# Step two of a staged transform: products laid out in PSUM with four frequencies side by side, and the fifth group's sums moved from VectorE to GpSimd

## The chip, the core and the metric

The kernel runs on one core of one Trainium2 chip. A core has five engines that run side by side, each with its own queue: TensorE (PE in the profile, with PEld for its weight loads), VectorE (DVE), ScalarE (ACT), GpSimd (POOL) and SyncE (SP, which here issues most DMAs). TensorE writes its results to PSUM; DVE and ACT read and write PSUM and SBUF; POOL is used on SBUF only. The metric is the device time of the whole program in microseconds (us), taken as the median of several runs; smaller is better.

## What is computed

The input is 2048 tokens by 640 channels. Two blocks are applied, each with a normalisation and a modulation ahead of it and a gated residual behind it. The change touches the first block only, a long causal convolution per channel that the reference does with an FFT:

```python
k_shift = sum over 4 taps of k_pad[:, t:t+S, :] * shift_k[:, ks-1-t]
kv  = k_shift * v
kv_f = rfft(pad(kv, S));  kf_f = rfft(pad(ssm_k, S))
y   = irfft(kv_f * kf_f)[:S] + kv * ssm_D
x   = x + ga * (h * y)          # h: normalised, modulated x
...
h = layernorm(x) * (1 + cb) + sb
x = x + gb * (w2^T gelu(w1^T layernorm(h) + b1) + b2)   # over the token axis
```

The product of the two spectra, `kv_f * kf_f`, is a complex product: for each frequency and channel, (a + ib)(c + id) gives a real part ac - bd and an imaginary part ad + bc.

## The kernel before

The second block (a token MLP, which fills the time from about 292 us on) is a long run of matmuls and is not touched. The first block goes over the channels in five chunks of 128 (the loop `for c in range(NC)`, line 524 on). In each chunk the transform of length 2048 is done as two small dense transforms, each a set of matmuls, and back again with two more:

- `step1(side, t)` (line 222): first transform, one call for each of four quarters t and for each of two sides (0: kv, 1: the filter). It writes PSUM, and ACT copies the result into the SBUF tile `T_z` (line 235).
- `f2(g)` (line 239): **step two**, called for eight groups g of eight frequencies k1. For each frequency (kk), each of two results (ri: real, imaginary) and each half h of the partitions there is one matmul at line 249: the weight is 128x64 from `W2`, the moving operand is 64 columns of `T_z` in 32 pairs, the pairs 1 KiB apart; of the 64 result columns the first 32 belong to kv (s = 0) and the last 32 to the filter (s = 1). That makes 32 matmuls a group, 256 a chunk and 1280 in the program; the profile has two MATMUL records and two LDWEIGHTS records for each (these operands are f32), so 64 a group, 512 a chunk, 2560 in all. The two halves h write different partitions of the same columns.
- Behind the matmuls of a group ACT copies the filter's part into an SBUF tile `kt` (line 253, one of two). `mul()` then makes two DVE instructions of 512 elements a partition: `pa` = kv's part times `kt`, `pb` = kv's part times `kt` with real and imaginary swapped. Both read kv's part straight from PSUM and write the SBUF tile `P`, whose two halves of 1024 serve even and odd groups. `add()` makes two instructions of 256 elements: a difference over `pa` for the real part, a sum over `pb` for the imaginary part, both written to `Y`.
- `i2(r)` (line 271) and `i1(half)` (line 289) transform back. `i2` reads `Y`, and so waits for the sums of all eight groups.

What sets the order around the change is the loop over g, written by hand. Iteration g issues the matmuls and the ACT copy of group g, then `mul` of group g - 1, then `add` of group g - 2, then some other DVE work (the four taps of a later chunk, `kv_ops`, one instruction at a time from a list). The sums go to POOL, with two exceptions. In chunks 2 and 3, iteration 6 gives its sums (those of group 4, the fifth of eight) to DVE. In chunks 1 to 4 the last group's sums are cut in two halves of 128 elements and go to DVE as well. Behind the loop stand two calls of `step1` for the next chunk, then `i2(0)`.

Two pools of storage tie the engines together. PSUM has three rotating buffers of 1024 words a partition (`psum()`, line 71), so the matmuls of group g + 3, or the next `step1`, can start only when both DVE products of group g have read theirs. And a half of `P` can be written by `mul` of group g only when the sums of group g - 2 have read it. All elementwise instructions of two inputs go through the helper at line 60, so in the profile they all carry that line, and are told apart by tile names: `p<-pst,kt` is a product, `y<-p` a sum, `kt<-in,tap`, `tap<-tap,kt` and `x<-tap,in` are the taps.

In the layout before, a matmul writes 64 neighbouring words. A group's 1024 words a partition are ordered (kk, ri, s, i) with i the 32 columns of a side, so ACT and DVE read PSUM in runs of 32 words, and the sums, which write `Y` as (i, k) with eight k in a row, read `P` one word at a time with 64 words (256 bytes) from one to the next.

Of the kernel before, what the change touches and what calls it, by code (L numbers as in the profile page):

```python
# [11 lines left out]
AF = mybir.ActivationFunctionType  # L12
ALU = mybir.AluOpType
# [37 lines left out]
def mixer_kernel(ctx: ExitStack, tc: tile.TileContext, q, k, v, shift_k, ssm_k, ssm_D, w1, b1, w2, b2, c,  # L51
# [7 lines left out]
    act, dve, pool, pe, sync = nc.scalar, nc.vector, nc.gpsimd, nc.tensor, nc.sync  # L59
    TT = lambda eng, o, a, b, op: eng.tensor_tensor(o, a, b, op=op)  # L60
    uid = [0]

    def mem(tag, n, name=None):

        return sb.tile([128, n], F32, name=name or tag, tag=tag, bufs=1)
# [5 lines left out]
    def psum(slot=None):  # L71

        uid[0] += 1
        slot = ring[uid[0] % len(ring)] if slot is None else slot
        return psp.tile([128, 1024], F32, name=f"pst_{uid[0]}", tag=f"pst{slot}", bufs=1)

    def dram(t, offset, ap):
        return bass.AP(tensor=t.tensor, offset=t.offset + offset, ap=ap)
# [20 lines left out]
    Y = T_y.rearrange("p (r i k) -> p r i k", r=2, i=32)  # L99
    W2 = [t.rearrange("p (k m) -> p k m", m=64) for t in T_w2]  # L100
# [6 lines left out]
    def lay_w2(i, n):  # L107

        k, e = slice(32 * (n // 2), 32 * (n // 2) + 32), n % 2
        act.activation(W2[i][:, k, 32 * e:32 * e + 32], W2C[i][:, k], AF.Copy, scale=MK[:, e:e + 1])  # L110
# [59 lines left out]
    def perm_add(c, eng=pool):  # L170
        for h in range(2):
            r = KSR[64 * h:64 * h + 1].rearrange("p (i n) -> p i n", i=64)[:, :, 0]
            TT(eng, r, r, DR[64 * h:64 * h + 1], ALU.add)
# [65 lines left out]
    def f2(g):  # L239

        ps = psum()
        for kk in range(8):
            k1 = 8 * g + kk
            for ri in range(2):
                for h in range(2):
                    o = 128 * kk + 64 * ri
                    rhs = bass.AP(tensor=T_z.tensor, offset=T_z.offset + 128 * h + 2 * k1,
                                  ap=[T_z.ap[0], [256, 32], [1, 2]])
                    pe.matmul(ps[64 * h:64 * h + 64, o:o + 64], W2[k1 // 32][:, 2 * (k1 % 32) + ri], rhs, start=True, stop=True)  # L249
        pv = ps.rearrange("p (m s i) -> p m s i", s=2, i=32)  # L250
        xs_ = pv[:, :, 0]
        kt = KT[g % 2]
        act.activation(kt.rearrange("p (m i) -> p m i", i=32), pv[:, :, 1], AF.Copy)  # L253
        pa, pb = P[:, 1024 * (g % 2):1024 * (g % 2) + 512], P[:, 1024 * (g % 2) + 512:1024 * (g % 2) + 1024]
        m16 = lambda t: t.rearrange("p (m i) -> p m i", i=32)

        def mul():
            TT(dve, m16(pa), xs_, m16(kt), ALU.mult)
            sw = bass.AP(tensor=kt.tensor, offset=kt.offset + 32, ap=[kt.ap[0], [64, 8], [-32, 2], [1, 32]])
            TT(dve, pb.rearrange("p (k r i) -> p k r i", k=8, r=2), xs_.rearrange("p (k r) i -> p k r i", r=2), sw,  # L260
               ALU.mult)

        def add(eng=pool, parts=(slice(0, 32),)):
            for i in parts:
                for ri, t, op in ((0, pa, ALU.subtract), (1, pb, ALU.add)):
                    t = t.rearrange("p (k r i) -> p r i k", k=8, r=2)
                    TT(eng, Y[:, ri, i, 8 * g:8 * g + 8], t[:, 0, i], t[:, 1, i], op)
        return mul, add


# [18 lines left out]
    def i1(half, slot=None):  # L289

        ps = psum(slot)
        for jj in range(8):
            for ri in range(2):
                for e in range(2):
                    p = slice(64 * e, 64 * e + 64)
                    for b in range(2):
                        n2 = 16 * b + 8 * half + jj
                        pe.matmul(ps[64 * b:64 * b + 64, 512 * e + 64 * jj:512 * e + 64 * jj + 64],  # L298
                                  V1[p, ri, n2], T2[p, :, 32 * ri + n2], start=ri == 0, stop=ri == 1)
        return ps  # L300
# [118 lines left out]
    def split_rows(r, t, blocks, hi=True, lo=True):  # L419
        j, t = slice(4 * r, 4 * r + 4), t.rearrange("p (j m) -> p j m", j=4)  # L420
        for f in blocks if hi else ():
            act.activation(blk[f][0][:, j].bitcast(F32R), t[:, :, 128 * f:128 * f + 128], AF.Copy)
        for f in blocks if lo else ():
            TT(dve, blk[f][1][:, j].bitcast(F32R), t[:, :, 128 * f:128 * f + 128], blk[f][0][:, j], ALU.subtract)
# [86 lines left out]
    def load_q():  # L511
        for j in range(16):
            for b in range(2):
                sync.dma_start(XH[j // 8][64 * b:64 * b + 64, j % 8], dram(q, (16 * b + j) * D, [[32 * D, 64], [1, D]]))
        for kk in range(4):
            mod_load(0, kk, (T_v1[:, 0:1920], T_v1[:, 1920:3840], T_aux[:, 0:1920], T_aux[:, 2048:3968])[kk])
# [3 lines left out]
    def dv(n):  # L520
        for _ in range(min(n, len(fill))):
            fill.pop(0)()

    x1s = lambda c, j: lambda: dve.bn_stats(bst[:, j, c, :], XR(j, DC * c, DC))
    for c in range(NC):
        cn = c + 1 if c + 1 < NC else None
        ac, po = a1_ops(c)
        pend_m = pend_a = None
        for g in range(8):
            m_, a_ = f2(g)  # L530
            if pend_m:
                pend_m()
            if pend_a:
                pend_a(dve if c in (2, 3) and g == 6 else pool)
            pend_a, pend_m = (pend_m and pa_next), m_
            pa_next = a_
            if c:
                for f_ in ac[2 * g:2 * g + 2]:
                    f_()
            if cn is None and g < 4:  # L540

                act.activation(X[:, 512 * g:512 * g + 1], epsc, AF.Copy)
                for b in range(2):
                    sync.dma_start(X[64 * b:64 * b + 64, 512 * g:512 * g + 512],
                                   dram(w1, (16 * b + g) * F, [[32 * F, 64], [1, 512]]))
            if c == 0 and g < 4:
                lay_w2(1, g)
                if g == 3:
                    load_q()
            if cn is None:  # L550
                dv(4 if g else len(fill) - 16)
                if g == 5:
                    t = mem("w0", 4096, "wb0")
                    blk[0] = j16(t[:, 0:2048]), j16(t[:, 2048:4096])
                if g in (5, 7):
                    split_rows(1, T_aux[:, 0:2048], (0,), g == 5, g == 7)
            else:
                dv(-(-len(fill) // max(6 - g, 1)))
            if c and cn is not None and g == 3:
                perm_add(cn)  # L560
# [16 lines left out]
        if c == 0:  # L577
# [3 lines left out]
            ps = psum()  # L581
# [45 lines left out]
        else:  # L627
            t = mem("w1", 4096, "wb1")
# [6 lines left out]
            t = mem("in", 4288, "wb3")  # L635
# [4 lines left out]
        if c:  # L640
# [3 lines left out]
            if cn is None:  # L644
# [5 lines left out]
                t = mem("y", 4096, "wb2")  # L650
# [20 lines left out]
        for half in range(2):  # L671
            ps = i1(half)
# [33 lines left out]
    start = []  # L706
# [91 lines left out]
    ps = i1(1, s1)  # L798
# [227 lines left out]
    for f_ in FS:  # L1026
# [12 lines left out]
        ps = psum().rearrange("p (h m) -> p h m", h=2)  # L1039
# [117 lines left out]
def build(inputs):  # L1157
    import concourse.bacc as bacc

    nc = bacc.Bacc("TRN2", target_bir_lowering=False, num_devices=1)  # L1160
    arrays, args = {}, []

    def add(name, a):
        a = np.ascontiguousarray(a)
        arrays[f"in_{name}_dram"] = a
        args.append(nc.dram_tensor(f"in_{name}_dram", a.shape, mybir.dt.from_np(a.dtype), kind="ExternalInput").ap())

    for name in _INS:
        a = np.asarray(inputs[name])
        add(name, a.reshape(S, D) if name in ('A_q', 'A_k', 'A_v') else a)  # L1170
    for name, a in _constants().items():
        add("const_" + name, a)
    args.append(nc.dram_tensor("out_0_dram", (S, D), F32, kind="ExternalOutput").ap())
    with tile.TileContext(nc) as tc:
        mixer_kernel(tc, *args)
    return nc, arrays
# [8 lines left out]
```

## Time and profile before

| what | value |
|---|---|
| median of 3 runs | 682.18 us (678.96 to 683.72) |
| the profiled execution, its own time | 679.36 us |
| its span, first to last instruction | 677.6 us |
| mean granted TensorE clock | 0.990 |
| busy: PE, DVE, ACT, POOL | 629.8, 513.0, 316.0, 143.4 us |
| the five chunks of the first block | about 23 to 292 us |

The profiled execution is 2.82 us below the median of the runs, and 1.76 us of its time lie outside the span. A line of the profile's groups gives line, engine, operation, output<-input tiles, partitions x elements and count, then the busy time, the mean duration in ns of one, and the idle time of the engine just before them with what ended it. A timeline line gives start, length, engine, line, operation, tiles, shape, count, and in brackets how long the engine had been idle before it and who released it. Matmul durations overlap, so the rate of matmuls is read from starts and stretches, not from the duration of one.

### The profile page before, as it was taken

What the parts mean: (1) busy time and instruction counts of PE and PEld (TensorE: products, weight loads), DVE (VectorE), ACT (ScalarE), POOL (GpSimd) and SP (SyncE); (2) the same over time, 40 slices, a digit from 0 to 9 for tenths busy, and PEclk for the clock granted to TensorE, in tenths of its full rate; (3) what the DMA queues carried; (4) which work ended last, traced back from release to release, by engine and by line L of the source; (5) the groups of instructions that cost most, each with busy time, mean ns of one, the idle gap of its engine ahead of it and who ended that gap; (6) DMA issues with size and microseconds to landing.
All of it is one profiled execution on the core that took longest, in us unless ns stands there. A gap on an engine that the chain in (4) does not pass through costs nothing.

```text
span 677.6 us, 20710 instructions
## 1 busy us (share of the span) xinstructions
PE 629.8 (93%) x9057; PEld 611.8 (90%) x9057; DVE 513.0 (76%) x862; ACT 316.0 (47%) x483; POOL 143.4 (21%) x116
## 2 busy tenths in 40 slices
PE   0699888999999999889999999999999999999997
PEld 0699678999989989668999999999999999999997
DVE  7677689979978757879993312854679888888886
ACT  0574674745645546557875223433334333333331
POOL 5298039526327228200000000000000000000000
PEclk9999989999999999979999999999999999999999
DMA  9977987655432522634005540686499554355601
GB/s 188 217 219 237 369 147 152 156 95 136 85 69 86 165 63 69 180 86 102 2 1 108 116 88 1 166 221 172 143 345 304 176 178 121 114 160 167 182 34 40
DMA packets 173552, 95.91 MB, mean 142 GB/s; under 512 B 89715, under 2 KB 163222, under 8 KB 173462
## 3 DMA queue, kind: packets, MB, share of 16 engines
q1 hardware_dynamic: 168914, 93.28, 52.9%
q10 hardware_dynamic: 4548, 1.31, 1.1%
q8 instruction: 71, 1.16, 0.7%
q14 instruction: 19, 0.16, 0.1%
HBM read 77.53 MB, written 17.04 MB: 140 GB/s over the span
## 4 chain that ended last, share of the span: by engine, by line
PE 69%; DVE 17%; POOL 3%; issue 3%; DMA 3%; SPq 3%; ACT 2%; ACTq 0%; DVEq 0%; POOLq 0%
PE pst L1086 25%; PE pst L445 17%; PE pst L230 9%; PE pst L249 6%; PE pst L279 5%; PE pst L951 3%; DVE tap L60 3%; PE pst L298 2%; POOL y L60 2%; DVE p L60 2%; DVE kt L60 2%; SPq L166 1%; DVE x L60 1%; DMA in<-in_A_k_dram 1%; POOL t L60 1%
## 5 line engine op out<-in xcount | busy, mean ns | idle before, releaser
L249 PEld LDWEIGHTS pst<-z,w 128*64 128x64 f32 x2560 | 94.8, 141 | 5.8 <-ACT z L235 3.3
L249 PE MATMUL pst<-z,w 128*64 128x64 f32 x2560 | 96.1, 240 | 4.1 <-ACT z L235 2.1
L60 POOL TENSOR_TENSOR y<-p 128x256 f32<-128x256 f32 x68 | 89.4, 1366 | 25.6 <-DVE p L60 25.3
L230 PE MATMUL pst<-v,x 128*64 128x128 f32 x640 | 46.0, 303 | 25.4 <-DVE x L60 23.3
L230 PEld LDWEIGHTS pst<-v,x 128*64 128x64 f32 x640 | 43.9, 220 | 26.2 <-POOL t L470 23.2
L235 ACT ACTIVATE z<-pst 128x1024 f32<-128x1024 f32 (+2 forms) x45 | 46.5, 1046 | 41.8 <-PE pst L230 24.1
L60 DVE TENSOR_TENSOR p<-pst,kt 128x512 f32<-128x512 f32 x80 | 52.0, 692 | 15.2 <-ACT kt L253 8.7
L253 ACT ACTIVATE kt<-pst 128x512 f32<-128x512 f32 x40 | 25.3, 633 | 44.7 <-PE pst L249 25.3
L279 PEld LDWEIGHTS pst<-v,y 32*128 32x128 f32 x1280 | 38.7, 190 | 5.8 <-issue 3.9
L279 PE MATMUL pst<-v,y 32*128 32x64 f32 x1280 | 40.4, 275 | 3.2 <-issue 2.3
L230 PE MATMUL pst<-v,p 128*64 128x128 f32 x640 | 36.7, 274 | 2.4 <-ACT p L176 1.8
L230 PEld LDWEIGHTS pst<-v,p 128*64 128x64 f32 x640 | 35.0, 137 | 2.9 <-ACT p L176 1.9
L1086 PE MATMUL pst<-r_z,m_w 128*128 128x320 f32 x198 | 37.2, 309 | 0.0
L60 DVE TENSOR_TENSOR tap<-tap,kt 128x512 f32<-128x512 f32 x51 | 35.6, 697 | 1.3
L60 DVE TENSOR_TENSOR kt<-in,tap 128x512 f32<-128x512 f32 x51 | 35.1, 688 | 1.5
L1086 PEld LDWEIGHTS pst<-r_z,m_w 128*128 128x128 f32 x198 | 31.1, 188 | 0.1
L287 ACT ACTIVATE z<-pst 128x512 f32<-128x512 f32 x38 | 21.4, 664 | 19.6 <-PE pst L279 19.5
L1023 ACT ACTIVATE m_w<-m_v 128x896 fp32r<-128x896 f32 x19 | 17.9, 948 | 23.2 <-DVE m_v L60 13.1
L298 PEld LDWEIGHTS pst<-z,v 64*64 64x64 f32 x1280 | 23.0, 148 | 5.3 <-issue 2.5
L298 PE MATMUL pst<-z,v 64*64 64x64 f32 x1280 | 24.8, 233 | 1.9 <-issue 1.1
L855 ACT ACTIVATE pst<-pst,sm 128x640 f32<-128x640 f32 x14 | 10.7, 766 | 32.5 <-PE pst L445 32.5
L60 DVE TENSOR_TENSOR m_w<-m_v,m_w 128x896 fp32r<-128x896 f32 x19 | 20.6, 1087 | 6.5 <-ACT m_w L1023 6.5
(302 smaller groups left out, 1435.5 us busy)
## 6 DMA issues: line engine op xcount, KB each, us to landing
x<-in_B_w_dram SPq DMA_DIRECT2D x18, 512.0 KB
m_v<-in_B_w_dram SPq DMA_DIRECT2D x20, 384.0 KB
aux<-in_A_ssm_k_dram SPq DMA_DIRECT2D x10, 512.0 KB
out_dram<-m_w SPq DMA_DIRECT2D x32, 160.0 KB
in<-in_A_k_dram SPq DMA_DIRECT2D x36, 128.0 KB
in<-in_A_v_dram SPq DMA_DIRECT2D x36, 128.0 KB
ts<-m_p SPq DMA_DIRECT2D x10, 320.0 KB
m_w<-xs SPq DMA_DIRECT2D x20, 160.0 KB
```

Of the source, the lines that this page charges most:

```text
L60: TT = lambda eng, o, a, b, op: eng.tensor_tensor(o, a, b, op=op)
L230: pe.matmul(ps[64 * ri:64 * ri + 64, o:o + 128], lhs, F1[:, 128 * ri:128 * ri + 128], start=True, stop=True)
L235: act.activation(Z[:, side, t, :, k0:k1].rearrange("p a k e -> p e a k"), ps.rearrange("p (e a k) -> p e a k", a=8, e=2)[:, :, :, k0:k1], ...
L249: pe.matmul(ps[64 * h:64 * h + 64, o:o + 64], W2[k1 // 32][:, 2 * (k1 % 32) + ri], rhs, start=True, stop=True)
L253: act.activation(kt.rearrange("p (m i) -> p m i", i=32), pv[:, :, 1], AF.Copy)
L279: pe.matmul(pp[qd // 2][:, o:o + 64], Y[p, ri, i:i + 2].rearrange("p i k -> p (i k)"), V2[p, 64 * ri:64 * ri + 64], start=ri == 0, stop=ri ...
L287: act.activation(o, i, AF.Copy)
L298: pe.matmul(ps[64 * b:64 * b + 64, 512 * e + 64 * jj:512 * e + 64 * jj + 64], V1[p, ri, n2], T2[p, :, 32 * ri + n2], start=ri == 0, stop=r ...
L445: pe.matmul(ps[0:m, h, 0:320], w_.bitcast(F32R), r_[:, 320 * h:320 * h + 320].bitcast(F32R), start=first and i == 0, stop=last and i == 2)
L951: pe.matmul(ps[n][:, h, 0:320], sets[n][:, j].bitcast(F32R), r[:, 320 * h:320 * h + 320].bitcast(F32R), start=j == 0 and r is hh, stop=j = ...
L1023: act.activation(W[n][0].bitcast(F32R), A[p, w_], AF.Copy)
L1086: pe.matmul(bank[n], w[:, i].bitcast(F32R), r.bitcast(F32R), start=m == 0 and k == 0, stop=m == 6 and k == 2)
```

## The change

The words of a group in PSUM are put in another order: (b, s, r, i, k), where b is the bank of 512 words, s the side, r real or imaginary, i the column, and k the four frequencies of that bank, innermost. Bank b holds the frequencies 4b to 4b + 3. A matmul now writes its 64 words one by one, four words (16 bytes) apart, in two rows of 32 that are 256 words apart. ACT and DVE read PSUM in runs of 256 words, the products lie in `P` in the same order, and the sums read `P` in runs of 128 words and write `Y` in runs of four words where they wrote runs of eight. The matmuls, their order, weights and moving operands stay as they are, and so do the number and size of the copies and products. The second edit takes the exception of chunks 2 and 3 out: group 4's sums go to POOL there too.

```diff
@@ f2(g)
         ps = psum()
+        pk = ps.rearrange("p (b s r i k) -> p b r k s i", b=2, s=2, r=2, i=32)
         for kk in range(8):
             k1 = 8 * g + kk
             for ri in range(2):
                 for h in range(2):
-                    o = 128 * kk + 64 * ri
                     rhs = bass.AP(tensor=T_z.tensor, offset=T_z.offset + 128 * h + 2 * k1,
                                   ap=[T_z.ap[0], [256, 32], [1, 2]])
-                    pe.matmul(ps[64 * h:64 * h + 64, o:o + 64], W2[k1 // 32][:, 2 * (k1 % 32) + ri], rhs, start=True, stop=True)
-        pv = ps.rearrange("p (m s i) -> p m s i", s=2, i=32)
+                    pe.matmul(pk[64 * h:64 * h + 64, kk // 4, ri, kk % 4], W2[k1 // 32][:, 2 * (k1 % 32) + ri], rhs,
+                              start=True, stop=True)
+        pv = ps.rearrange("p (b s m) -> p b s m", b=2, s=2)
         xs_ = pv[:, :, 0]
         kt = KT[g % 2]
-        act.activation(kt.rearrange("p (m i) -> p m i", i=32), pv[:, :, 1], AF.Copy)
+        halves_ = lambda t: t.rearrange("p (b m) -> p b m", b=2)
+        act.activation(halves_(kt), pv[:, :, 1], AF.Copy)
         pa, pb = P[:, 1024 * (g % 2):1024 * (g % 2) + 512], P[:, 1024 * (g % 2) + 512:1024 * (g % 2) + 1024]
-        m16 = lambda t: t.rearrange("p (m i) -> p m i", i=32)
         def mul():
-            TT(dve, m16(pa), xs_, m16(kt), ALU.mult)
-            sw = bass.AP(tensor=kt.tensor, offset=kt.offset + 32, ap=[kt.ap[0], [64, 8], [-32, 2], [1, 32]])
-            TT(dve, pb.rearrange("p (k r i) -> p k r i", k=8, r=2), xs_.rearrange("p (k r) i -> p k r i", r=2), sw,
+            TT(dve, halves_(pa), xs_, halves_(kt), ALU.mult)
+            sw = bass.AP(tensor=kt.tensor, offset=kt.offset + 128, ap=[kt.ap[0], [256, 2], [-128, 2], [1, 128]])
+            TT(dve, pb.rearrange("p (b r m) -> p b r m", b=2, r=2), xs_.rearrange("p b (r m) -> p b r m", r=2), sw,
                ALU.mult)
         def add(eng=pool, parts=(slice(0, 32),)):
             for i in parts:
                 for ri, t, op in ((0, pa, ALU.subtract), (1, pb, ALU.add)):
-                    t = t.rearrange("p (k r i) -> p r i k", k=8, r=2)
-                    TT(eng, Y[:, ri, i, 8 * g:8 * g + 8], t[:, 0, i], t[:, 1, i], op)
+                    t = t.rearrange("p (b r i k) -> p r b i k", b=2, r=2, i=32)[:, :, :, i]
+                    TT(eng, Y[:, ri, i, 8 * g:8 * g + 8].rearrange("p i (b k) -> p b i k", b=2), t[:, 0], t[:, 1], op)
@@ loop over g
             if pend_a:
-                pend_a(dve if c in (2, 3) and g == 6 else pool)
+                pend_a()
```

What moves can be seen on two engines. On DVE, at the end of step two of chunk 2 before the change, where pst_2296, 2337, 2384 and 2424 are the PSUM buffers of groups 4 to 7:

```order
L60 TENSOR_TENSOR p<-pst_2296,kt 128x512 x2
L60 TENSOR_TENSOR x<-tap,in 128x512
L60 TENSOR_TENSOR p<-pst_2337,kt 128x512 x2
L60 TENSOR_TENSOR y<-p 128x32x8 x2
L60 TENSOR_TENSOR p<-pst_2384,kt 128x512 x2
L60 TENSOR_TENSOR p<-pst_2424,kt 128x512 x2
L60 TENSOR_TENSOR y<-p 128x16x8 x4
```

The same place on DVE after the change:

```order
L60 TENSOR_TENSOR p<-pst_2296,kt 128x512 x2
L60 TENSOR_TENSOR x<-tap,in 128x512
L60 TENSOR_TENSOR p<-pst_2337,kt 128x512 x2
L60 TENSOR_TENSOR p<-pst_2384,kt 128x512 x2
L60 TENSOR_TENSOR p<-pst_2424,kt 128x512 x2
L60 TENSOR_TENSOR y<-p 128x2x16x4 x4
```

Group 4's two sums no longer stand between the products of groups 5 and 6, and the last group's four half sums keep their place with another shape. On POOL, chunk 2 from the end of chunk 1's additions to its own sums, before the change (aux<-aux,rows is a small addition of one row, the rest y<-p are sums):

```order
L60 TENSOR_TENSOR xa<-xa,aux 128x8x128
L60 TENSOR_TENSOR xb<-xb,aux 128x8x128
L60 TENSOR_TENSOR y<-p 128x32x8 x4
L60 TENSOR_TENSOR aux<-aux,rows 1x64 x2
L60 TENSOR_TENSOR y<-p 128x32x8 x8
```

The same place on POOL after the change:

```order
L60 TENSOR_TENSOR xa<-xa,aux 128x8x128
L60 TENSOR_TENSOR xb<-xb,aux 128x8x128
L60 TENSOR_TENSOR y<-p 128x2x32x4 x4
L60 TENSOR_TENSOR aux<-aux,rows 1x64 x2
L60 TENSOR_TENSOR y<-p 128x2x32x4 x10
```

POOL has two sums more in the chunk, ten in place of eight behind the small addition; chunk 3 moves alike, and POOL has 72 sums in the program in place of 68.

## The prediction

> **What bounds the kernel now.** I read the page's busy times first, then the five stretches of step two, then what TensorE waits for around them, then the timeline at one of those waits. The page's first part says that TensorE is busy nearly all the time:
>
> ```profile
> PE 629.8 (93%) x9057; PEld 611.8 (90%) x9057; DVE 513.0 (76%) x862; ACT 316.0 (47%) x483; POOL 143.4 (21%) x116
> ```
>
> That share is a mean over stages, so the next view is line 249 alone in its five stretches, chunk by chunk (stretch; its length; PE and weight-load busy time with counts; clock; DMA share; GB/s):
>
> ```profile
> 41.24:60.20 18.96, 18.96 (x512) 18.90 (x512) 1.00 0.80 228
> 102.26:124.12 21.86, 19.84 (x512) 19.18 (x512) 1.00 0.78 160
> 152.84:171.70 18.86, 18.86 (x512) 18.86 (x512) 1.00 0.55 132
> 202.03:220.90 18.87, 18.87 (x512) 18.87 (x512) 1.00 0.35 103
> 251.92:270.90 18.98, 18.98 (x512) 18.91 (x512) 1.00 0.29 80
> ```
>
> In four of the five stretches busy time equals length: TensorE runs step two's 512 records back to back in 18.9 us, at full clock, and is the bound there. Only chunk 1 has holes, 21.86 - 19.84 = 2.02 us. So neither the sums on POOL nor the products on DVE set the pace of step two now. They can cost time only where TensorE waits, and these are all of its waits from 100 to 290 us (us in total, times, longest):
>
> ```profile
> PE pst L279 <- issue: 2.3, 1, 2.3
> PE pst L230 <- DVE p L60: 2.1, 2, 1.1
> PE pst L249 <- DVE p L60: 2.0, 3, 0.7
> PE pst L249 <- ACT z L235: 1.7, 4, 0.4
> PE pst L298 <- issue: 1.1, 2, 0.9
> PE pst L230 <- PE pst L298: 0.6, 1, 0.6
> PE pst L279 <- DVE y L60: 0.3, 1, 0.3
> ```
>
> They add up to 10.1 us, 1.5% of the run. Everything that the change can give back lies in this list, and mostly in the rows that name DVE. The timeline at the end of chunk 2's step two shows the second row at work:
>
> ```profile
> 169.63 0.62 ACT L253 ACTIVATE kt<-pst 128x512 f32<-128x512 f32 x1 [0.91 <-PE pst L249]
> 170.33 0.69 DVE L60 TENSOR_TENSOR p<-pst,kt 128x512 f32<-128x512 f32 x1 [0.61 <-POOL y L60]
> 170.94 2.70 DVE L60 TENSOR_TENSOR y<-p 128x256 f32<-128x256 f32 x2
> 171.71 2.26 PE L230 MATMUL pst<-v,x 128*64 128x128 f32 x32
> 171.98 0.61 ACT L253 ACTIVATE kt<-pst 128x512 f32<-128x512 f32 x1 [0.96 <-PE pst L249]
> 173.56 2.47 DVE L60 TENSOR_TENSOR p<-pst,kt 128x512 f32<-128x512 f32 x4
> 174.32 2.18 POOL L60 TENSOR_TENSOR y<-p 128x256 f32<-128x256 f32 x2 [1.20 <-DVE p L60]
> 174.99 2.28 PE L230 MATMUL pst<-v,x 128*64 128x128 f32 x32 [1.02 <-DVE p L60]
> 175.96 1.73 DVE L60 TENSOR_TENSOR y<-p 128x128 f32<-128x128 f32 x4
> 177.20 1.01 PE L279 MATMUL pst<-v,y 32*128 32x64 f32 x28
> ```
>
> Group 6's filter part was in `kt` at 170.25, but DVE took group 4's two sums first, until 173.56, and only then the products of group 6. The second `step1` needs that group's PSUM buffer and stands 1.02 us.
>
> **The change part by part.** *The sums.* The groups that price them, before the change and for data in one run:
>
> ```profile
> L60 POOL TENSOR_TENSOR y<-p 128x256 f32<-128x256 f32 x68 | 89.4, 1366 | 25.6 <-DVE p L60 25.3
> L60 POOL TENSOR_TENSOR t<-t 128x512 f32<-128x512 f32 x9 | 11.7, 1297 | 0.7
> L60 POOL TENSOR_TENSOR xa<-xa,aux 128x1024 f32<-128x1024 f32 x3 | 7.2, 2389 | 49.9 <-DVE aux L60 49.9
> L60 DVE TENSOR_TENSOR y<-p 128x128 f32<-128x128 f32 x16 | 8.6, 595 | 0.0
> L60 DVE TENSOR_TENSOR y<-p 128x256 f32<-128x256 f32 x4 | 5.4, 1394 | 0.0
> L60 DVE TENSOR_TENSOR x<-tap,in 128x512 f32<-128x512 f32 x17 | 11.8, 691 | 5.3 <-PE pst L230 4.9
> L60 DVE TENSOR_TENSOR aux<-pst,aux 128x1024 f32<-128x1024 f32 x9 | 10.9, 1220 | 13.5 <-PE pst L298 13.5
> ```
>
> On POOL a sum of 256 elements takes 1366 ns, more than 512 elements in runs (1297). From 512 to 1024 elements in runs an element costs (2389 - 1297)/512 = 2.13 ns, so 256 would take 1297 - 256 x 2.13 = 751 ns. The writes stay short (runs of four where they were eight), so my bounds are 751 and 1366 (no row says that the writes cost anything; above 1366 only if they did, a rival below). I take 800: the reads are what the change turns into runs. POOL then has 72 x 0.8 = 58 us in place of 89.4, none of it on the path. On DVE an element in runs costs (1220 - 691)/512 = 1.03 ns, so a half sum would take 691 - 384 x 1.03 = 295 ns in place of 595: 16 x 0.3 = 4.8 us less, and the four full sums, 5.4 us, leave DVE. That is 10 us of DVE time, off the path except where TensorE waits.
>
> *The path, chunk 2.* With the sums gone and no wait for POOL, the products of group 6 start when `kt` is there, at 170.3, and end by 171.7; those of group 7 follow its copy (171.98 + 0.61) from 172.6 to 174.0. The second `step1` starts when the first ends, at 173.97, so its 1.02 us go. Next in line is `i2`: it needs group 7's buffer (174.0), the last half sums (174.0 + 4 x 0.3 = 175.2), POOL's sums of group 6 (171.7 + 2 x 0.8 = 173.3, behind group 5's) and TensorE itself, free at 173.97 + 2.28 = 176.25. TensorE is last, so nothing takes the place of the wait: -1.02 us. Group 4's sums on POOL need 1.6 us that it has, since it now works 10 x 0.8 us where it worked 8 x 1.37.
>
> *Chunks 3 and 4.* The same wait in chunk 3, and a small one for the last sums in chunk 4:
>
> ```profile
> 224.24 2.28 PE L230 MATMUL pst<-v,x 128*64 128x128 f32 x32 [1.08 <-DVE p L60]
> 275.04 3.58 PE L279 MATMUL pst<-v,y 32*128 32x64 f32 x120 [0.33 <-DVE y L60]
> ```
>
> -1.08 us and -0.33 us. Chunk 0 has no wait of this kind. Chunk 1's 2.02 us stay: there DVE had no sums to take and no gap, its products were late behind the taps, and neither moves. The copies and products keep their size; their 512 elements already cost DVE 1.03 ns each from runs of 32, so longer runs bring nothing: 0.
>
> *The matmuls.* This is the term that decides. A record of line 249 now writes its 64 words singly, 16 bytes apart, and no matmul in this trace does that. 512 records in 18.87 us, two at a time on the two halves of the partitions, are 73.7 ns for 64 words, 1.15 ns a word. The nearest rows are matmuls that write runs faster, and a weight load that reads single words:
>
> ```profile
> 364.25 2.80 PE L445 MATMUL pst<-r_z,wb0b 128*128 128x320 f32 x18
> 366.89 2.80 PE L445 MATMUL pst<-r_v,wb0b 128*128 128x320 f32 x18
> 146.94 5.46 PE L230 MATMUL pst<-v,p 128*64 128x128 f32 x96
> ```
>
> Line 445 writes 18 x 320 words in 366.89 - 364.25 = 2.64 us, 0.458 ns a word, so two neighbours every 0.92 ns. If a single word costs as much as two neighbours, 64 of them take 59 ns, less than the 73.7 that the matmul needs anyway: +0. At the other end are single words read from SBUF: line 230 with `x`, whose weights lie 32 words apart, runs 32 records in 2.26 us, 141 ns for two side by side, against 5.46/96 x 2 = 114 ns with `p`, whose weights lie in a run. Taken whole, 141/64 = 2.2 ns a word, so 64 words would take 141 ns: (141 - 73.7) x 1280 = +86 us. Below nothing is excluded: weights and moving words stay as they are, and scattered writes have no reason to be faster than a run. I take 0, since line 445 is the row on PSUM itself and the other is on SBUF; the ends are 0 and +86 us.
>
> [...]
>
> **Sum.** -1.02 - 1.08 - 0.33 + 0 = -2.43 us: 679.36 becomes 676.9 for an execution like the profiled one. That one lies 2.82 us below the median, so on the median's scale 682.18 - 2.43 = 679.7 us.
>
> **The rivals.** *First, slower: scattered writes bound step two.* Place: the five stretches, where TensorE has no slack. It decides from 1.15 ns a word on. If a lone word takes the time of four neighbours (its 16 bytes), 4 x 0.458 = 1.83 ns, a record pair takes 117 ns, (117 - 73.7) x 1280 = +56 us, 679.7 + 56 = 736; at the SBUF price 679.7 + 86 = 766. For it: single words are slow in this very trace (141 against 114 ns in line 230; 1394 against 691 - 256 x 1.03 = 427 ns for a sum on DVE). Against it: PSUM takes twice as many words in the same time from line 445, and a price of up to two neighbours hides. *Second, a little slower:* 1.2 to 1.3 ns a word, 77 to 83 ns a pair, +4 to +12 us: 684 to 692. *Third, faster by more than 1%:* DVE's 10 us also clear the rest of the waits, chunk 1's 2.02 us and the 2.3 us ahead of line 279 in chunk 4: -2.4 - 2.0 - 2.3 = -6.7, 675.5. Against it: nothing in chunk 1 moves, and the 2.3 us name no other engine. *Fourth, the sums don't get faster,* because runs of four on the write side hold POOL: then two more sums of 1.37 us end POOL's work in chunks 2 and 3 at about 176.5 + 2.7 = 179.2, past TensorE's 177.2, +2 us each and the gain gone: 686.
>
> **How the numbers follow.** A measurement of this kernel tells about 1% from no change. Forecast 0.57 (677 to 683 by the spread of the runs); first rival 0.25; second 0.09; third 0.06; fourth 0.03. Faster by over 1% comes from the third alone and the forecast's edge, 0.07; slower by over 1% from the first and second, 0.34; the rest, 0.59, is within 1%. The range starts below the third at 675. Without the first rival 0.75 would be in, so it reaches up to that rival's lower case, 736, which takes in about half of it.
>
> **What would show it.** The five stretches of line 249: 18.9 us each if I am right, 24 to 30 us if scattered writes cost. The sums on POOL near 0.8 us and on DVE near 0.3 us. The waits of line 230 for DVE's products in chunks 2 and 3 gone, chunk 1's three still there. I am wrong if the stretches are longer, or if they stay and the time still moves by over 7 us.

## The result and the profile after

| what | before | after |
|---|---|---|
| median of 6 runs each, on one chip | 682.01 us (678.96 to 683.72) | 678.32 us (677.43 to 679.74) |
| ratio of the times | | 0.9948 (95% interval 0.9924 to 0.9971) |
| the profiled execution, its own time | 679.36 us | 678.04 us |
| its span; mean granted clock | 677.6 us; 0.990 | 676.2 us; 0.987 |

The changed kernel is half a per cent faster, by an interval that lies below 1, and within the 1% that the forecast called no change. The forecast was 679.7 us. Ratios here and below leave out the few executions that ran more than 1.5% longer than the shortest of their kernel, while medians and ranges hold them. In the changed kernel the numbers of the lines from the end of `f2` on are higher by one or two: the copy to `kt` is line 255, `i2` line 280, `i1` line 299, the token MLP line 446.

First the busy times of the page of after:

```profile
PE 629.5 (93%) x9057; PEld 612.5 (91%) x9057; DVE 502.5 (74%) x858; ACT 315.8 (47%) x483; POOL 109.4 (16%) x120
```

TensorE's busy time is what it was (629.8), DVE's is 10.5 us less and POOL's 34 us less although it has four instructions more. The whole gain in time must then be TensorE's idle time. The five stretches of line 249 in after, columns as before (stretch; length; PE and weight-load busy time with counts; clock; DMA share; GB/s):

```profile
41.30:60.20 18.90, 18.87 (x512) 18.87 (x512) 1.00 0.79 228
105.36:125.20 19.84, 19.44 (x512) 19.05 (x512) 1.00 0.81 163
154.40:173.30 18.90, 18.89 (x512) 18.89 (x512) 1.00 0.62 147
202.00:220.90 18.90, 18.89 (x512) 18.89 (x512) 1.00 0.41 124
250.58:269.56 18.98, 18.98 (x512) 18.88 (x512) 1.00 0.30 80
```

Writing the words singly, 16 bytes apart, costs these matmuls nothing that shows: 18.9 us for 512 records, as before, busy from end to end in four chunks. The groups of sums, products and copies in after (out<-in, partitions x elements, count; busy time, mean ns of one; idle before them):

```profile
L60 DVE TENSOR_TENSOR p<-pst,kt 128x512 f32<-128x512 f32 x80 | 51.4, 687 | 16.4 <-POOL y L60 10.7 <-ACT kt L255 5.5
L60 POOL TENSOR_TENSOR y<-p 128x256 f32<-128x256 f32 x72 | 53.9, 774 | 46.1 <-DVE p L60 45.9
L60 DVE TENSOR_TENSOR y<-p 128x128 f32<-128x128 f32 x16 | 3.5, 282 | 0.0
L255 ACT ACTIVATE kt<-pst 128x512 f32<-128x512 f32 x40 | 25.2, 630 | 42.9 <-PE pst L249 21.6 <-ACT aux L306 11.4 <-DVE p L60 3.1
```

A sum takes 774 ns on POOL where it took 1366, and a half sum 282 ns on DVE where it took 595 in the mean (that mean mixes two cases, which the experiment with sums done twice takes apart). TensorE's waits from 100 to 290 us in after (us in total, times, longest):

```profile
PE pst L280 <- issue: 2.6, 1, 2.6
PE pst L249 <- ACT z L235: 1.7, 4, 0.4
PE pst L299 <- issue: 1.3, 2, 0.9
PE pst L249 <- DVE p L60: 0.4, 1, 0.4
PE pst L230 <- PE pst L299: 0.3, 1, 0.3
```

The row of line 230 for DVE's products (2.1 us) and the row for the last sums (0.3 us) are gone. The timeline of after at the end of chunk 2's step two shows the place where the first of them stood (start, length, engine, line, tiles, count, idle before):

```profile
171.22 0.62 ACT L255 ACTIVATE kt<-pst 128x512 f32<-128x512 f32 x1 [0.94 <-ACT aux L306]
171.94 1.29 DVE L60 TENSOR_TENSOR p<-pst,kt 128x512 f32<-128x512 f32 x2 [1.03 <-POOL y L60]
173.32 4.20 PE L230 MATMUL pst<-v,x 128*64 128x128 f32 x63
173.57 0.60 ACT L255 ACTIVATE kt<-pst 128x512 f32<-128x512 f32 x1 [0.97 <-ACT aux L306]
174.27 1.29 DVE L60 TENSOR_TENSOR p<-pst,kt 128x512 f32<-128x512 f32 x2 [1.03 <-POOL y L60]
175.47 0.89 DVE L60 TENSOR_TENSOR y<-p 128x128 f32<-128x128 f32 x4
177.44 3.80 PE L280 MATMUL pst<-v,y 32*128 32x64 f32 x128
```

Group 6's products start at 171.94, 0.10 us after their copy has ended (171.22 + 0.62); before, 2.70 us of sums lay between the two. Both calls of `step1` now run as one piece, and from their start to `i2` it is 177.44 - 173.32 = 4.12 us, where it was 177.20 - 171.71 = 5.49 us: 1.37 us less, the 1.02 us of the wait and 0.35 us more. Those 0.35 us are the break itself: the two calls took 2.26 and 2.21 us around the wait and take 4.12/2 = 2.06 us each in one piece. DVE is done at 176.4 and TensorE is last, as the prediction had it.

The two profiled executions differ by 1.4 us of span, less than the medians, because a load of chunk 1 landed later in the one of after. The DVE chain of chunk 1 in before:

```profile
99.91 0.70 DVE L60 TENSOR_TENSOR tap<-in,tap 128x512 f32<-128x512 f32 x1 [0.78 <-DMA in<-in_A_k_dram]
...
128.38 0.89 PE L279 MATMUL pst<-v,y 32*128 32x64 f32 x23
```

and in after:

```profile
101.04 0.69 DVE L60 TENSOR_TENSOR tap<-in,tap 128x512 f32<-128x512 f32 x1 [1.79 <-DMA in<-in_A_k_dram]
...
129.47 0.79 PE L280 MATMUL pst<-v,y 32*128 32x64 f32 x20
```

From the first tap behind the load to `i2` it is 28.47 and 28.43 us: chunk 1 goes at the pace of that chain and not of TensorE, and starts when the load lands. So the two executions are best laid side by side by the time from step two's first matmul to `i2`'s first:

| us from step two to `i2` | chunk 0 | 1 | 2 | 3 | 4 |
|---|---|---|---|---|---|
| before | 27.08 | 26.12 | 24.36 | 24.42 | 22.34 |
| after | 27.09 | 24.12 | 23.03 | 23.02 | 22.34 |

Chunk 1's 2.00 us are not won: there step two started 3.10 us later (105.36 against 102.26) and the chain's end moved by 1.09 us. Chunks 2 and 3 give 1.33 and 1.40 us. In chunk 4 the first half of `i2`, up to the next matmuls (line 362, after: 363), runs 3.73 us in place of 4.29. The wait of 0.33 us is gone from it, and 0.56 us are won.

### The profile page after: what moved, and what is told of

It reads as the page before. It is cut to its first block, busy times and chain, and to the rows that moved or that the text cites. A ratio compares the mean times of both kernels' runs of the same rounds, so it can differ in the third digit from the quotient of the medians.

```text
span 676.2 us, 20710 instructions
## 1 busy us (share of the span) xinstructions
PE 629.5 (93%) x9057; PEld 612.5 (91%) x9057; DVE 502.5 (74%) x858; ACT 315.8 (47%) x483; POOL 109.4 (16%) x120
## 4 chain that ended last, share of the span: by engine, by line
PE 84%; DVE 7%; SPq 3%; DMA 2%; issue 1%; ACT 1%; ACTq 0%; DVEq 0%
PE pst L1087 25%; PE pst L446 24%; PE pst L249 12%; PE pst L230 11%; PE pst L280 5%; PE pst L952 3%; PE pst L299 2%; DVE tap L60 2%; DVE kt L60 2%; SPq L166 2%; PE tap L363 1%; DMA in<-in_A_k_dram 1%; SPq L144 1%; DMA m_v<-in_B_w_dram 1%; DVE x L60 1%
## 5 line engine op out<-in xcount | busy, mean ns | idle before, releaser
L60 POOL TENSOR_TENSOR y<-p 128x256 f32<-128x256 f32 x72 | 53.9, 774 | 46.1 <-DVE p L60 45.9
L230 PE MATMUL pst<-v,p 128*64 128x128 f32 x640 | 38.6, 281 | 3.1 <-ACT p L176 2.8
L230 PEld LDWEIGHTS pst<-v,p 128*64 128x64 f32 x640 | 36.7, 142 | 3.8 <-ACT p L176 3.0
L288 ACT ACTIVATE z<-pst 128x512 f32<-128x512 f32 x38 | 21.4, 663 | 19.7 <-PE pst L280 19.6
L299 PEld LDWEIGHTS pst<-z,v 64*64 64x64 f32 x1280 | 21.6, 140 | 5.8 <-issue 3.1
L446 PE MATMUL pst<-r_z,wb 128*128 128x320 f32 x144 | 23.5, 324 | 3.5 <-ACT r_z L762 3.5
L446 PEld LDWEIGHTS pst<-r_z,wb 128*128 128x128 f32 x144 | 22.9, 200 | 3.8 <-ACT r_z L762 3.8
L299 PE MATMUL pst<-z,v 64*64 64x64 f32 x1280 | 23.3, 226 | 2.5 <-issue 1.8
```

The source lines that it names most:

```text
L230: pe.matmul(ps[64 * ri:64 * ri + 64, o:o + 128], lhs, F1[:, 128 * ri:128 * ri + 128], start=True, stop=True)
L288: act.activation(o, i, AF.Copy)
L446: pe.matmul(ps[0:m, h, 0:320], w_.bitcast(F32R), r_[:, 320 * h:320 * h + 320].bitcast(F32R), start=first and i == 0, stop=last and i == 2)
```

## The experiments

My theory was that the time comes from the shorter sums alone, that the order of a bank costs a matmul nothing because its f32 words come no faster than PSUM takes lone ones, and that the second edit is not needed. The rivals: the gain comes from the move of the fifth sums to POOL; matmuls are held a little by the scattered words, and more by another distance; the new order helps the copies and products too. "The kernel before" is run beside every timed experiment on the same chip; ratios are against it.

**The fifth sums back on DVE, in the new order** (of the changed kernel):

```diff
-                pend_a()
+                pend_a(dve if c in (2, 3) and g == 6 else pool)
```

> The new layout, with group 4's sums of chunks 2 and 3 given back to VectorE. Theory (the layout itself removes the waits, since a sum from runs is short): the two sums cost VectorE about 2 x 0.43 us where they cost 2 x 1.35, the products of group 6 still end before the second step1 needs their buffer, no wait of line 230 for products comes back, and the time is that of the changed kernel within 0.3 us, about 3 us under the kernel before. Rival (the move off VectorE brings the gain): the waits of about 1 us in chunks 2 and 3 come back and the time is about 2 us above the changed kernel.

Measured: 679.56 us (677.84 to 684.30, 12 runs) beside 681.96 (29 runs), ratio 0.9983 (0.9962 to 1.0003; that of the two medians, 0.9965, lies inside). From step two to `i2` chunks 2 and 3 take 23.11 and 23.02 us, as in the changed kernel. The group of the four sums on DVE, and the timeline at the end of chunk 2's step two:

```profile
L60 DVE TENSOR_TENSOR y<-p 128x256 f32<-128x256 f32 x4 | 3.0, 790 | 0.0
```

```profile
169.67 1.51 DVE L60 TENSOR_TENSOR y<-p 128x256 f32<-128x256 f32 x2
171.10 1.27 DVE L60 TENSOR_TENSOR p<-pst,kt 128x512 f32<-128x512 f32 x2
172.14 4.31 PE L230 MATMUL pst<-v,x 128*64 128x128 f32 x64
176.38 1.89 PE L280 MATMUL pst<-v,y 32*128 32x64 f32 x58
```

The two sums end at 171.18, 1.51 us after they began where they took 2.70 us, and `step1` runs as one piece: the wait does not come back. So the order of the words takes it away without the move. A sum on DVE took 790 ns and not the 0.43 us that I had from the slope of longer sums; POOL's sums run beside all four. The interval of the ratio overlaps the changed kernel's (0.9924 to 0.9971) and holds 1, so the times alone neither give the move a share nor deny it one; the trace gives it none at this place.

**The move without the new order** (of the kernel before):

```diff
-                pend_a(dve if c in (2, 3) and g == 6 else pool)
+                pend_a()
```

> The old layout, with all fifth sums on GpSimd. Theory (the move alone is no gain, the sums are too slow there): GpSimd has ten sums of 1.37 us behind its small addition in chunks 2 and 3 and ends them some 2 us past the point where TensorE could begin the backward transform, so line 279 waits for GpSimd's sums there, and the time is 1 to 4 us above the kernel before. Rival (the move brings the gain): chunks 2 and 3 lose their waits for products as in the changed kernel, 2 us under the kernel before.

Measured: 685.81 us (682.42 to 691.70, 11 runs) beside 681.96, ratio 1.0056 (1.0032 to 1.0080): slower. The group of the sums, TensorE's wait, and the timeline at the end of chunk 2's step two:

```profile
L60 POOL TENSOR_TENSOR y<-p 128x256 f32<-128x256 f32 x72 | 92.7, 1336 | 25.0 <-DVE p L60 24.7
```

```profile
PE pst L279 <- DVE y L60: 2.7, 5, 0.8
```

```profile
167.29 10.82 POOL L60 TENSOR_TENSOR y<-p 128x256 f32<-128x256 f32 x9
172.59 4.23 PE L230 MATMUL pst<-v,x 128*64 128x128 f32 x63
176.46 2.47 DVE L60 TENSOR_TENSOR y<-p 128x128 f32<-128x128 f32 x4
177.28 0.45 PE L279 MATMUL pst<-v,y 32*128 32x64 f32 x8 [0.46 <-DVE y L60]
...
178.48 1.78 PE L279 MATMUL pst<-v,y 32*128 32x64 f32 x55 [0.75 <-DVE y L60]
```

The wait of line 230 for the products is gone here as well, and chunks 2 and 3 take 23.60 and 23.59 us to `i2`. But nine sums stand in a row on POOL until 178.11, and the last half sums on DVE begin at 176.46 and take 2.47 us, past the 176.82 at which TensorE is done with `step1`. `i2` starts late and breaks off, and from its start to the next step two chunk 2 takes 25.84 us (24.83 before). What is won ahead of `i2` is lost in it. This is close to the fourth rival's mechanism, at the price that sums would have if they had not become shorter; but I had expected `i2` to wait for POOL's sums, and the matmuls' wait names DVE's half sums. POOL holds those up: beside its last sums the first two take 682 and 1277 ns, behind them the other two 369 and 372 ns. The rest of the 0.56% is not taken apart: chunk 2 is only 0.2 us longer in all, and in chunk 3, which is 1.6 us longer, the granted clock is 0.53 from 230 to 237 us, where it is 1.00 in the profile of before.

**Eight frequencies side by side.** A bank holds one result (real or imaginary) of all eight frequencies, k innermost, so a matmul writes words 32 bytes apart and the sums read and write runs of eight or more:

```diff
-        pk = ps.rearrange("p (b s r i k) -> p b r k s i", b=2, s=2, r=2, i=32)
+        pk = ps.rearrange("p (r s i k) -> p r k s i", r=2, s=2, i=32)
-                    pe.matmul(pk[64 * h:64 * h + 64, kk // 4, ri, kk % 4], W2[k1 // 32][:, 2 * (k1 % 32) + ri], rhs,
+                    pe.matmul(pk[64 * h:64 * h + 64, ri, kk], W2[k1 // 32][:, 2 * (k1 % 32) + ri], rhs,
...
-                    t = t.rearrange("p (b r i k) -> p r b i k", b=2, r=2, i=32)[:, :, :, i]
+                    t = t.rearrange("p (r i k) -> p r i k", r=2, i=32)[:, :, i]
```

> One PSUM bank for the real and one for the imaginary part, so that eight frequencies lie side by side: a matmul of step two writes single words 32 bytes apart, sums write runs of eight. Theory (a single word costs TensorE about as much as two neighbours, wherever the next one lies): five stretches of line 249 of 18.9 us as before, sums on GpSimd of 0.70 to 0.77 us, the time that of the changed kernel within 0.5 us. Rival (what counts is the distance, 16 bytes being one line): the stretches grow to 24 to 30 us, and the time by 25 to 55 us.

Measured: 679.87 us (677.18 to 682.22, 12 runs) beside 681.96, ratio 0.9968 (0.9950 to 0.9987). Line 249 in chunk 2, and the sums:

```profile
155.12:174.00 18.88, 18.88 (x512) 18.88 (x512) 1.00 0.61 144
```

```profile
L60 POOL TENSOR_TENSOR y<-p 128x256 f32<-128x256 f32 x72 | 54.0, 773 | 46.7 <-DVE p L60 46.4
```

Twice the distance costs the matmuls nothing (18.88 us), and writes in runs of eight do no more for the sums than runs of four (773 ns against 774). Whether its time is within 0.5 us of the changed kernel's, as expected, the runs can't tell: the intervals of the two ratios overlap.

**The price of a lone word by itself.** Spare matmuls were added to the changed kernel behind the first block, and their results are overwritten. Each form has 48 matmuls of 512 bf16 words, or 32 of f32 in the form of line 249 (128 x 64 weights, 64 records, the matmuls on the two halves of the partitions in turn). Line 811 writes a run, lines 813, 815 and 817 single words 8, 16 and 32 bytes apart (k = 2, 4, 8), line 819 pairs of words 16 bytes from one to the next; line 821 writes f32 in a run, 823 and 825 singly, 16 and 32 bytes apart:

```diff
+    for i in range(48):
+        pe.matmul(t16(i), ob, mv16, start=True, stop=True)
+    for i in range(48):
+        pe.matmul(t16(i).rearrange("p (i k) -> p k i", k=2), ob, mv16, start=True, stop=True)
...
+    for i in range(48):
+        pe.matmul(t16(i).rearrange("p (i k e) -> p k i e", k=2, e=2), ob, mv16, start=True, stop=True)
+    for i in range(32):
+        pe.matmul(t32(i), ones, mv32, start=True, stop=True)
+    for i in range(32):
+        pe.matmul(t32(i).rearrange("p (i k) -> p k i", k=4), ones, mv32, start=True, stop=True)
...
```

> The changed kernel with eight groups of spare matmuls ahead of the 24 that already stand before the token MLP; their results are overwritten, nothing of the computation is left out. Five groups of 48 in bf16 with 512 words each, written as a run, singly 8, 16 and 32 bytes apart, and in pairs of neighbours 16 bytes apart; three groups of 32 in f32 with 512 words on half the partitions, as a run, singly 16 and 32 bytes apart. Theory (a lone word takes the slot of a pair of neighbours): bf16 0.42 to 0.46 ns a word as a run and in pairs, 0.83 to 0.92 ns singly at any distance; f32 the same for all three groups, since a word leaves only every 0.83 to 0.9 ns anyway. First rival (a line of 16 bytes): bf16 singly 16 bytes apart 1.8 ns, 8 bytes apart half of it, f32 singly twice the run. Second rival (scattered writes cost nothing here at all): all bf16 groups alike, all f32 groups alike.

One execution with a profile; its time of 800.16 us holds the added matmuls. Its timeline, one row a form; the time of a form is read from its start to the next one's:

```profile
298.92 12.28 PE L811 MATMUL pst<-sm 128*128 128x512 bf16 x48 [1.68 <-ACT kt L388]
311.04 20.76 PE L813 MATMUL pst<-sm 128*128 128x512 bf16 x48
331.60 20.80 PE L815 MATMUL pst<-sm 128*128 128x512 bf16 x48
352.20 20.80 PE L817 MATMUL pst<-sm 128*128 128x512 bf16 x48
372.80 10.66 PE L819 MATMUL pst<-sm 128*128 128x512 bf16 x48
383.39 14.13 PE L821 MATMUL pst<-sm 128*64 128x512 f32 x64
397.35 14.08 PE L823 MATMUL pst<-sm 128*64 128x512 f32 x64
411.26 14.08 PE L825 MATMUL pst<-sm 128*64 128x512 f32 x64
425.26 3.78 PE L827 MATMUL pst<-wb,wb 128*128 128x320 f32 x24
```

The granted clock in these stretches is 1.00 but for the first, whose row of the busy times by windows (stretch; length; PE, PEld, DVE, ACT, POOL busy with counts; clock; DMA share; GB/s) is:

```profile
299.00:311.00 12.00, 12.00 (x48) 4.98 (x48) 11.20 (x31) 8.15 (x18) 0.00 (x0) 0.86 0.57 127
```

| form | start to start, us | ns a word |
|---|---|---|
| bf16, run | 12.12 (clock 0.86 at its start) | 0.493 |
| bf16, pairs, 16 bytes from one to the next | 10.59 | 0.431 |
| bf16, singly, 8 bytes apart | 20.56 | 0.837 |
| bf16, singly, 16 and 32 bytes apart | 20.60, 20.60 | 0.838 |
| f32, run | 13.96 | 0.852 |
| f32, singly, 16 and 32 bytes apart | 13.91, 14.00 | 0.849, 0.854 |

DVE and ACT work beside the first forms and hardly beside lines 817 to 825 (DVE is busy 19.6 us beside line 813 and 2.9 us beside line 817), which makes no difference between lines 813 and 817 (20.56 and 20.60 us). (ns a word: the time by 48 x 512 for bf16; by 32 x 512 for f32, whose 32 matmuls have two records each.) A lone word has a price, 1.94 times that of a word in a pair, and it is the same at 8, 16 and 32 bytes (0.837 to 0.838 ns). It is just the price of two neighbours (2 x 0.431 = 0.862). An f32 matmul of this form brings a word every 0.85 ns to a run or not, so that price is hidden entirely; line 249, whose matmuls have only 64 words, needs 1.15 ns and has room on top. The pairs are not contiguous either and take 0.431 ns a word, no more than the run (0.493 at its clock of 0.86). So in these rows single words cost time only where words come faster than one in 0.84 ns.

**The changed kernel again**, with no edit, beside the kernel before:

> The changed kernel as it is, beside the kernel before and the two kernels below on one chip. Theory (three waits of TensorE go, worth 1.0 to 1.4 us in chunks 2 and 3 and 0.3 to 0.6 in chunk 4, and nothing else changes): ratio 0.995 to 0.997. Rival (the layout brings more, in chunk 1 too): 0.992 or less.

Measured: 678.96 us (676.30 to 681.43, 12 runs) beside 682.04 (23 runs), ratio 0.9933 (0.9906 to 0.9961). The ratio lies between the theory's 0.995 and the rival's 0.992, and its interval holds both. In the trace chunks 2 to 4 are as in the first profile of the changed kernel (23.02, 23.11 and 22.34 us from step two to `i2`), and chunk 1 has no gain. Its profile also answers a question on chunk 1, with TensorE's waits of line 249 for products from 100 to 290 us:

```profile
PE pst L249 <- DVE p L60: 2.8, 4, 0.7
```

All four lie in chunk 1, 0.68 to 0.71 us each, where the first profile of the changed kernel has one of 0.38 us and that of before has three, 2.0 us together. They come and go with the moment at which step two starts against the chain of taps, and not with the change: step two starts 1.32 us behind the chain's first tap here, 2.35 us in before and 4.32 us in the first profile of after, and the later it starts the less it waits (2.8, 2.0 and 0.4 us). The kernel with the move alone and the old order falls where after does (4.37 and 0.4 us).

**Every sum on POOL twice**, the second writing the same values again (of the changed kernel):

```diff
-                    TT(eng, Y[:, ri, i, 8 * g:8 * g + 8].rearrange("p i (b k) -> p b i k", b=2), t[:, 0], t[:, 1], op)
+                    for _ in range(2 if eng is pool else 1):
+                        TT(eng, Y[:, ri, i, 8 * g:8 * g + 8].rearrange("p i (b k) -> p b i k", b=2), t[:, 0], t[:, 1], op)
```

> The changed kernel, with each sum on GpSimd done twice (same inputs, same output, so the result stays), which makes a group's sums there about as long as in the layout before, 3.1 us. Theory (what the layout brings is the length of the sums and nothing else): GpSimd falls behind again, the products wait for it, TensorE waits ahead of the backward transform in chunks 2 and 3, and the time is 1 to 5 us above the kernel before, like the old layout with all fifth sums on GpSimd. Rival (longer runs for the products and copies bring the gain): still 1 to 3 us under the kernel before.

Measured: 706.08 us (704.72 to 708.13, 4 runs) beside 682.04, ratio 1.0330 (1.0272 to 1.0388). The group of the sums, and TensorE's waits over the whole span (here `i2` is line 281):

```profile
L60 POOL TENSOR_TENSOR y<-p 128x256 f32<-128x256 f32 x144 | 107.2, 764 | 32.4 <-DVE p L60 26.4
```

```profile
PE pst L281 <- POOL y L60: 11.6, 8, 2.4
...
PE pst L230 <- DVE p L60: 3.3, 5, 0.7
...
PE pst L249 <- DVE p L60: 2.7, 4, 0.7
```

The direction was expected, the size not: 24 us over the kernel before. Two sums in place of one are 2 x 0.764 = 1.53 us, only 0.16 us longer than the sum of before, but there DVE took group 4's. Chunk 2 has 14 sums on POOL in the changed kernel: doubled they take 14 x 1.53 = 21.4 us, longer than the 18.9 us that TensorE needs for step two, so POOL becomes the bound of the stage. In the experiment that moved the sums alone it had 14 x 1.336 = 18.7 us, just under, and lost 4 us. Waits of TensorE that name POOL or DVE explain 17.6 us here; which part of the rest is the lower clock (0.960) was not taken apart. The changed kernel has 14 x 0.774 = 10.8 us, far from this bound.

The same trace tells something on DVE. Its half sums, which this edit does not touch, in before (with the four full sums) and here (ns: shortest/median/longest, then first and last start in us):

```profile
L60 DVE TENSOR_TENSOR y<-p x20: 369/552/1626, 126.4 to 275.1; 128x128 f32<-128x128 f32 x16, 128x256 f32<-128x256 f32 x4
L60 DVE TENSOR_TENSOR y<-p x16: 277/544/818, 132.4 to 300.8; 128x128 f32<-128x128 f32 x16
```

In the changed kernel POOL's sums are over by then, but for the end of one in chunk 1, and each half sum takes 279 to 284 ns. Here all sixteen overlap with POOL's sums, and of each four the middle two take 807 to 818 ns. Before the change, ten of the sixteen half sums had no sum of POOL beside them and took 369 to 403 ns, 380 in the mean, and the other six took 700 to 1336 ns. So the mean of 595 ns was not the price of words that lie 256 bytes apart: that is 380 against 282 ns, and the rest came with POOL's sums. Why POOL's sums lengthen these instructions is not shown; products and taps take 0.69 to 0.70 us in the mean here, beside them too.

**The gather at the read of PSUM** (of the kernel with eight side by side). Matmuls write runs of 64 as before; ACT's copy and DVE's products read PSUM one word at a time, 512 bytes apart, and write `kt` and `P` in runs with the eight frequencies side by side. So, against the kernel before, the matmuls are as they were, and the layout is turned by the reads (the views of `kt` and `P` follow):

```diff
-        pk = ps.rearrange("p (r s i k) -> p r k s i", r=2, s=2, i=32)
+        pk = ps.rearrange("p (k r m) -> p r k m", k=8, r=2)
-        pv = ps.rearrange("p (b s m) -> p b s m", b=2, s=2)
-        xs_ = pv[:, :, 0]
+        pv = ps.rearrange("p (k r s i) -> p s r i k", k=8, r=2, s=2)
+        xs_ = pv[:, 0]
```

> TensorE writes runs as before the change; ScalarE's copy and VectorE's products read PSUM word by word, 128 words from one to the next, and write the sums' order (real or imaginary, column, eight frequencies), so that the sums still read runs. Theory (a lone word costs a PSUM port about 0.85 ns, which TensorE's f32 words and VectorE's 1.04 ns an element both hide): copies of 0.63 us, products of 0.69 us and sums of 0.77 us as in the changed kernel, and its time within 0.5 us. Rival (VectorE's and ScalarE's reads of lone words cost as on SBUF, where a sum of 256 took 1394 ns against 427): products of 1.0 us and more, 80 of them 25 us longer on VectorE, and the time 5 to 15 us above the kernel before.

Measured: 679.00 us (676.84 to 690.30, 10 runs) beside 682.04, ratio 0.9953 (0.9937 to 0.9970). The groups:

```profile
L60 DVE TENSOR_TENSOR p<-pst,kt 128x512 f32<-128x512 f32 x80 | 51.3, 686 | 16.2 <-POOL y L60 10.3 <-ACT kt L255 5.7
L60 POOL TENSOR_TENSOR y<-p 128x256 f32<-128x256 f32 x72 | 53.9, 773 | 43.3 <-DVE p L60 42.9
L255 ACT ACTIVATE kt<-pst 128x512 f32<-128x512 f32 x40 | 25.0, 626 | 44.7 <-PE pst L249 21.6 <-ACT aux L305 9.4 <-DVE p L60 6.8
```

Lone words 512 bytes apart cost DVE's and ACT's reads of PSUM nothing (686 and 626 ns; 687 and 630 in the changed kernel with runs of 256 words). The gain is there with the matmuls writing as they did before. So the words' order in PSUM has no part in it; what has is that the sums' operands in SBUF lie in runs. The times of the changed kernel, of this one and of the one with eight side by side do not differ by more than their intervals.

## Why the prediction was right, point by point

- *Bound.* TensorE, with only its waits to win: right. Its busy time stayed (629.8 and 629.5 us), and DVE's 10.5 us and POOL's 34 us less show in the time only where TensorE had waited.
- *The sums.* 0.8 us on POOL and 0.3 us on DVE forecast, 0.774 and 0.282 measured. The slope of longer sums in runs gave the right price on POOL, and on DVE where POOL has no sum beside it. For the sums that went back to DVE in the first experiment it was wrong, 790 ns against 427, and POOL's sums run beside all four. That POOL's sums slow DVE's is shown by the half sums (282 ns, and 807 to 818 for half of them where only POOL's work beside them differs). The prediction therefore read two of its rows wrongly: all the sums of 1394 ns on DVE, and six of the sixteen behind the 595 ns, had POOL's sums beside them, so neither is the price of single words. The wait of 0.33 us in chunk 4 followed two half sums of 700 and 1308 ns of this kind; how much of its going is owed to POOL's earlier end, and how much to the half sums' own runs, is not taken apart. On POOL the words of a sum lay 256 bytes apart before the change, and a sum took 1366/774 = 1.76 times as long as with its words in runs (1062 ns for the shortest, 1.37 times).
- *The path in chunks 2, 3 and 4.* -1.02, -1.08 and -0.33 us forecast; -1.33, -1.40 and -0.56 us measured. The mechanism held: the wait went and TensorE was last at `i2`. The terms were sized too small by 0.2 to 0.3 us each, because I took the wait alone and not the break in the matmuls around it. By the runs the change is worth 682.01 - 678.32 = 3.7 us and, in the second set, 682.04 - 678.96 = 3.1 us; the three terms as measured make 3.3 us, as forecast 2.4. Half a per cent is less than the spread of single executions (678.96 to 683.72 us in before), so the account rests on the traces more than on the medians.
- *Chunk 1.* "Chunk 1's three still there" failed as it was put: the profile of after has one wait of 0.38 us, the repeat has four. The reason given, that its products are late behind the taps and neither moves, holds by the 28.4 us from load to `i2` in both kernels. The error was to expect a number of waits where the load sets how much of the chain's length TensorE sees as waiting.
- *The matmuls.* 0 taken, between 0 and +86 us: 0 measured, and the reason (a lone word costs at most two neighbours) is shown by the spare matmuls, 0.838 against 0.862 ns. My reading of the row of line 445 was luckier than it was safe: that row gives the price of two neighbours in a run, and that a lone word costs no more than both was assumed, which no row of before could show. Where words come faster, as the spare bf16 ones at 0.43 ns do, the same price does not hide (0.838 ns a word). The scattered read of weights, the upper end, says nothing of PSUM.
- *The rivals.* The first and second fall by the stretches of 18.9 us. The third falls, since chunk 1's chain (28.4 us) and the 2.6 us ahead of line 280 stayed. Sums that are too long on POOL do cost time, as the move without the new order shows at +0.56%, though the matmuls then wait for DVE's half sums beside them. The fourth's condition did not hold: writes in runs of four and of eight give 774 and 773 ns.
- *The second edit,* which I had summed with the first, is not needed for the gain on the path and harms without the first; a share of its own, up to some 0.35% by the two ratios (0.9983 and 0.9948), stays open.

## What to carry to other kernels

When one engine is busy 93% of the time, list its waits and price the change by them, plus a few tenths of a microsecond (0.2 to 0.3 here) for each stream of matmuls that is no longer broken off; what other engines save beyond that is not time. Before moving work to a helper engine, multiply its instructions in the stage by their duration and compare with the stage's length: 10.8 us of 18.9 was free, 18.7 cost 4 us and 21.4 cost 24 us. If a layout must be turned somewhere, turn it where a slower step hides it: here the writes of f32 matmuls (18.9 us a chunk in runs or singly) or the reads of PSUM (a product took 686 ns singly, 687 in runs), and not the reads of SBUF by the sums (1366 ns on POOL against 774).

## What the runs showed that I had not expected

- A lone word from a bf16 matmul costs PSUM 0.838 ns, whether 8, 16 or 32 bytes from the last; words in pairs cost 0.431 ns each, even with gaps between the pairs.
- f32 matmuls with 128 x 64 weights bring a word every 0.85 ns, run or not (0.849 to 0.854). Whether both of the records that stand for one of them write PSUM is not shown.
- DVE and ACT read lone PSUM words 512 bytes apart at the pace of runs (686 and 626 ns for 512 elements), while words 256 bytes apart in SBUF made a sum on POOL 1.76 times as long in the mean (1366 against 774 ns) and a half sum on DVE, with no sum of POOL beside it, 1.35 times (380 against 282 ns).
- POOL's sums slow DVE's: a half sum in runs takes 282 ns alone and up to 818 ns beside them, one in single words 380 and up to 1336 ns. A change that shortens POOL's sums can so shorten DVE's too.
